# Fewer, longer loads of the first queries, and a new deal of decoding and narrow copies between VectorE and ScalarE, in a causal attention with an MLP behind it

## The chip, the cores and the metric

One core of a Trainium2 chip runs the whole program. Its engines are TensorE (PE in the rows; PEld is its weight load), VectorE (DVE), ScalarE (ACT), GpSimd (POOL) and SyncE (SP), which here only issues transfers (SPq). The metric is device time in microseconds (us), median of several runs; lower is better. A measurement of this kernel can tell about 0.2% (1.2 us) from no change.

## The reference

```
scores = q @ k^T / sqrt(64), causal mask            # batch 4, heads 12, seq 448, dim 64
attn   = softmax(scores);  x = attn @ v             # -> 1792 tokens x 768
h = x @ w_in                                        # 768 x 2048
g = max(h, 0) + alpha * min(h, 0)
out = g @ w_out                                     # 2048 x 768
```

Everything is float32. The weights and v reach the kernel as 64-bit words, so w_in has to be decoded on the chip.

## The kernel before, in words

**Attention** works on 24 pairs of heads (p = 0 to 23). A loop of iterations n runs the steps of several pairs side by side: in iteration n a step written `NAME+lag` in the text `ORDER` (or in `ROUNDS` for the first n) is done for pair n - lag. The text is the order in which every engine's instructions are issued, and each engine takes its own in that order. The steps of one pair:

- `LK`, `LQ` (`load`): SP's loads of keys and queries, two transfers each, one for each head of the pair. The first 64 query rows go into a tile of their own, `qd` (two more transfers). `LW` loads `vd`, the v rows for the 64-row half blocks; `LV` loads pieces of v. `ST` stores finished x.
- `S0`, `S1`, `S2` (`scores`): TensorE. `MXij` (`row_max`): VectorE, mask and row extreme in PSUM. `EXij` (`row_exp`): ScalarE. `RC` (`row_rec`, the lines `sm` and `rs` in the rows): VectorE's reciprocal of the row sums. `NOij` (`row_norm`): the seven scalings on GpSimd, which start when RC is done.
- `PT0` to `PT2`, and `PTH` (`transpose_halves`, the half blocks): transposes on TensorE into PSUM. `C00` to `C30` (`pt_copy`): copies of them to SBUF. The last letter says which engine copies: a ScalarE, d VectorE. `C00` and `C30` are the narrow ones (128x256).
- `AV`, `AH`: attention times v on TensorE; `AH` needs `C30`. `XF`, `XH`, `XL`: sums and splits of x out of PSUM.

`E2`, `EH`, `EG`, `ED`, `EA` are places in the order at which other work is run, taken from the table `EARLY`, which has a list for each n. The words of it: `LD` loads a piece of w_in (SP, into one buffer `raw`, free again when the piece before is decoded); `A`, `I` (ScalarE), `C` (GpSimd), `D` (VectorE: `p_shift` and `p_sign`) and `+` (GpSimd, in two halves) decode piece 0, 1, 2; `S`, `cast`, `sub` make weight operands; `h` and `l` split x into a high part (GpSimd) and a low part (VectorE, line L725); `4` is a GpSimd sum. Most of them run at `ED`, near the end of the iteration; `A`, `I` and `cast` at `EA`, after it; `D` at `EG`, ahead of `XF` and `RC`.

**The MLP** starts inside the last iterations (`begin_block`, `go_on`, `last_of_it` of the hooks) and then runs as a planned list, with TensorE busy throughout.

Of the kernel before, what the change touches and what calls it, by code (L numbers as in the profile page):

```python
# [11 lines left out]
F32 = mybir.dt.float32  # L12
# [181 lines left out]
def kernel(  # L194
# [269 lines left out]
    def load(p, nm, eng=nc.sync, also=None):  # L464

        b, hp = pairs[p]
        o = LQ if nm == "q" else 0
        T[nm, p] = ap["in"].tile([P, S - o], F32, tag=nm + "r", name=f"{nm}r_{p}")
        src = {"q": qt, "k": kt}[nm][b, hp]
        for j in range(2):  # L470
            (also if j and also else eng).dma_start(out=T[nm, p][half(j)], in_=src[:, j, o:])
        if nm == "q":
            for j in range(2):
                eng.dma_start(out=qd[p % 3][half(j), j * LQ : (j + 1) * LQ], in_=src[:, j, :LQ])

# [60 lines left out]
    def scores(p, n):  # L536

        if n == 2:  # L540
# [94 lines left out]
    def pt_copy(p, i, j, eng):  # L635
# [290 lines left out]
    with tc.manual_schedule():  # L926
# [601 lines left out]
```

## Time and profile before

| | |
|---|---|
| median of 3 runs | 596.08 us (595.0 to 596.35) |
| the profiled execution | 596.71 us, of which the span from first to last instruction is 594.9 |
| PE busy, whole span | 571.3 us, 96% |
| DVE, ACT, POOL busy | 464.9, 393.0, 288.8 us |
| mean granted TensorE clock | 0.983 of 2.4 GHz |

A row of the timeline reads: start in us, length in us, engine, line, operation, what it writes and reads, how many of its kind are merged in it, and in square brackets how long the engine was idle before it and what ended that.

### The profile page before, as it was taken

To read this page: it belongs to the slowest core of one execution; us is meant where nothing else is said; L and a number is where in the kernel's file an instruction comes from. 1 tells how busy PE (TensorE), PEld (TensorE's weight loads), DVE (VectorE), ACT (ScalarE), POOL (GpSimd) and SP (SyncE) were. 2 spreads that over 40 slices of the span, in tenths; PEclk is the share of its full clock that TensorE was granted. 3 is DMA by queue.
4 is the path that set the end of the run, shared out by engine and by line. 5 is a ranking of instruction groups with operands and counts; after the bars stand their busy time and mean duration, and the time that the engine had idled before them with its cause. 6 is when DMAs were issued, how large, how long until landed. Compare 5 with 4: busy or idle time off the path is not lost.

```text
span 594.9 us, 11547 instructions
## 1 busy us (share of the span) xinstructions
PE 571.3 (96%) x3921; PEld 504.6 (85%) x3921; DVE 464.9 (78%) x975; ACT 393.0 (66%) x921; POOL 288.8 (49%) x334
## 2 busy tenths in 40 slices
PE   8998799879998999999999999999989999999997
PEld 4766567556687999999999999999979999999997
DVE  5886688858966977767886778887997899897763
ACT  6886889759967757556664754777676566565431
POOL 7665378777662434435444531533444453456420
PEclk9899799979999999999999999999999999999999
DMA  5755554553233676575676757395452325403533
GB/s 153 193 154 134 133 142 132 163 143 98 82 89 136 215 235 222 216 252 212 214 255 210 231 205 249 128 333 194 125 151 71 105 66 150 141 9 118 178 100 113
DMA packets 94586, 95.92 MB, mean 161 GB/s; under 512 B 24608, under 2 KB 83648, under 8 KB 94528
## 3 DMA queue, kind: packets, MB, share of 16 engines
q1 hardware_dynamic: 93680, 93.65, 51.0%
q0 software_dynamic: 528, 1.08, 0.7%
q8 instruction: 31, 0.51, 0.4%
q10 hardware_dynamic: 320, 0.46, 0.2%
q14 instruction: 27, 0.22, 0.1%
HBM read 66.85 MB, written 28.31 MB: 160 GB/s over the span
## 4 chain that ended last, share of the span: by engine, by line
PE 64%; DVE 4%; issue 1%; ACT 0%; DVEq 0%
PE bank L406 33%; PE bank L1321 30%; DVE x1l L1299 1%; DVE dec L1289 1%; DVE x1h L1258 0%; DVE dec L1247 0%; DVE wo L1258 0%; DVE tf L1289 0%; DVE acc L1457 0%; DVE wie L1258 0%; DVE acc L323 0%; PE bank L657 0%; DVE acc L1289 0%; DVE tf L1334 0%; DVE acc L319 0%
## 5 line engine op out<-in xcount | busy, mean ns | idle before, releaser
L528 POOL TENSOR_SCALAR p<-p,rs 128x192 f32<-128x192 f32 (+3 forms) x164 | 86.1, 546 | 54.9 <-DVE rs L599 35.9
L1321 PE MATMUL bank<-x1h,x1l 128*128 128x384 f32 x540 | 98.7, 335 | 1.0 <-DVE x1h L1258 0.9
L1321 PEld LDWEIGHTS bank<-x1h,x1l 128*128 128x128 f32 x540 | 94.3, 188 | 1.6 <-DVE x1h L1258 1.2
L585 ACT ACTIVATE p<-bank,nm 128x320 f32<-128x320 f32 (+3 forms) x168 | 82.1, 496 | 18.1 <-DVE nm L570 18.0
L570 DVE CUSTOM_DVE_ANT_0 bank<-bank,mask 128x320 f32<-128x320 f32 (+3 forms) x168 | 72.3, 478 | 22.0 <-ACT p L585 12.4
L430 ACT ACTIVATE tf<-bank 128x448 f32<-128x448 f32 x64 | 34.4, 543 | 41.9 <-PE bank L406 30.5
L557 PE MATMUL bank<-kr,qr 64*128 64x320 f32 (+2 forms) x288 | 51.7, 471 | 0.5 <-ACT x1h L524 0.5
L434 DVE SCALAR_TENSOR_TENSOR tf<-tf,om,bank 128x448 f32<-128x448 f32 x64 | 41.7, 674 | 7.7 <-ACT tf L430 7.3
L406 PE MATMUL bank<-x1h,wir 128*128 128x448 f32 x192 | 44.6, 368 | 0.0
L630 PE MATMUL bank<-ident,p 128*128 128x128 f32 x288 | 40.9, 294 | 1.4 <-POOL p L528 1.3
L1321 PE MATMUL bank<-x1h,gset 128*128 128x384 f32 x216 | 40.4, 338 | 0.9 <-DVE acc L1334 0.9
L524 ACT ACTIVATE ptf<-bank 128x384 f32<-128x384 f32 (+1 forms) x94 | 38.9, 470 | 2.0 <-PE bank L630 1.6
L649 PE MATMUL bank<-ptf,v 128*64 128x128 f32 (+2 forms) x288 | 35.7, 382 | 3.8 <-DMA v<-in_v_dram 3.8
L1321 PEld LDWEIGHTS bank<-x1h,gset 128*128 128x128 f32 x216 | 37.9, 188 | 1.2 <-ACT acc L1455 1.2
L406 PEld LDWEIGHTS bank<-x1h,wir 128*128 128x128 f32 x192 | 36.0, 188 | 3.3
L630 PEld LDWEIGHTS bank<-ident,p 128*128 128x128 f32 x288 | 33.9, 149 | 4.6 <-POOL p L528 2.8
L557 PEld LDWEIGHTS bank<-kr,qr 64*128 64x128 f32 x288 | 28.8, 198 | 10.6 <-ACT p L585 3.2
L329 POOL TENSOR_TENSOR dec<-dec,tf 128x768 int32<-128x768 int32 x11 | 22.0, 1996 | 30.6 <-ACT tf L430 16.5
L420 DVE TENSOR_TENSOR bank<-bank,tf 128x448 f32<-128x448 f32 x30 | 18.9, 630 | 22.1 <-PE bank L406 20.9
L1299 POOL TENSOR_TENSOR x1l<-acc,x1l 128x512 fp32r<-128x512 f32 x12 | 16.4, 1368 | 40.6 <-ACT x1l L1295 31.7
L585 ACT ACTIVATION_READ_ACCUMULATOR p<-bank,nm 128x1 f32 x168 | 33.7, 201 | 0.0
L406 PE MATMUL bank<-x1h,wie 128*128 128x448 f32 x144 | 33.4, 367 | 0.0
(195 smaller groups left out, 1387.1 us busy)
## 6 DMA issues: line engine op xcount, KB each, us to landing
gd<-tf SPq DMA_DIRECT2D x64, 224.0 KB, 2.1
tf<-gd SPq DMA_DIRECT2D x28, 256.0 KB, 4.5
acc<-gd SPq DMA_DIRECT2D x28, 256.0 KB, 4.3
dec<-in_moe_w_in_dram SPq DMA_DIRECT2D x9, 768.0 KB, 4.9
tf<-in_moe_w_in_dram SPq DMA_DIRECT2D x7, 768.0 KB, 4.8
dec<-in_moe_w_out_dram SPq DMA_DIRECT2D x7, 768.0 KB, 4.7
tf<-in_moe_w_out_dram SPq DMA_DIRECT2D x7, 768.0 KB, 4.6
dec<-wd SPq DMA_DIRECT2D x13, 384.0 KB, 4.6
```

The costliest lines, as they stand in the source:

```text
L406: nc.tensor.matmul(ps, w[:, u, k * P : (k + 1) * P], x[:, k], start=(st in ("P1", "P5") and i == 0), stop=(i == len(mms) - 1), skip_group_ ...
L430: nc.scalar.activation(t, bank_of(g, b, role), AF.Relu, scale=-1.0)
L434: stt(out=t, in0=t, scalar=om[:, f : f + 1], in1=bank_of(g, b, role), op0=ALU.mult, op1=ALU.add)
L524: eng.activation(out, x, AF.Copy, scale=side)
L528: eng.tensor_scalar(out=out, in0=x, scalar1=side, scalar2=1.0, op0=ALU.mult, op1=ALU.mult)
L557: nc.tensor.matmul(ps[:, o : o + lim], T["q", p][half(j), i * QP : (i + 1) * QP], T["k", p][half(j), :lim], start=(o == 0), stop=(n > 0 or ...
L570: nc.vector.tensor_tensor_reduce(out=t, in0=t, in1=mask_of(i), scale=-SCALE, scalar=MOST_F32, op0=ALU.add, op1=ALU.min, accum_out=nm,)
L585: nc.scalar.activation(T["p", p, i][:, j, : t.shape[1]], t, AF.Exp, scale=-1.0, bias=T.pop(("nm", p, i, j)), accum_out=T["sm", p][:, z : z ...
L630: nc.tensor.transpose(ps[:, j - js[0], c], t[:, j, c * QP : (c + 1) * QP], T["ident"])
L649: nc.tensor.matmul(out[half(j), c * QP + LQ :], vs[b % 2][:, hp, c, j], x[:, : (NQ - c) * QP], start=(c == 0), stop=False, skip_group_chec ...
L1299: eng.tensor_tensor(out=x[:, 4 * P :], in0=g_of(p, nm), in1=x[:, : 4 * P], op=ALU.subtract)
L1321: nc.tensor.matmul(ps, x, w, start=(st in ("P1", "P5")[: 1 if Q else 2] and i == 0), stop=(i == len(mms) - 1), skip_group_check=True,)
```

## The change

1. `load`: the first queries of three pairs come in one pair of transfers, at every third pair, into one of two larger `qd` tiles, instead of two transfers for every pair. On SP 16 rows of two transfers go away.
2. `p_sign` may work on half a piece (`G`), and each half stands in the iteration of its `+`. Pieces 0 and 1 are decoded about one iteration later; the second `LD` moves from n = 8 to n = 9, and its `A` from 9 to 10. `S`, `l` and all of `D`, `G` now run at `EG`, ahead of `XF` and `RC`.
3. `attention`: in twelve iterations `C00`, and in five of these `C30` too, is copied by VectorE instead of ScalarE. Early `LW` and `MX1` move behind other steps.
4. For the last pair (p = 23) `PTH` runs in n = 26 with its other transposes, in a bank it shares with PT0, and VectorE copies its `C30` there.

```
-    4: "A:0", 5: "I:0 C:0", 6: "D:0", 7: "D:0 +:0:0", 8: "+:0:1 LD", 9: "A:1", 10: "I:1 C:1", 11: "D:1 h", 12: "D:1 h l",
-    13: "+:1:0 h", 14: "+:1:1 4 h LD", 15: "4 h", 16: "S:S1 S:S2 l 4 h", 17: "S:S3 l l h cast:A11", 18: "l l h sub:A11 cast:S1",
-    19: "sub:S1 l h cast:S2", 20: "sub:S2 l h A:2", 21: "S:S4 l h C:2", 22: "l h I:2", 23: "l", 24: "l",
+    4: "A:0", 5: "I:0 C:0", 7: "D:0", 8: "G:0:0 +:0:0", 9: "G:0:1 +:0:1 LD", 10: "A:1", 11: "I:1 C:1 h", 12: "h", 13: "D:1 h",
+    14: "G:1:0 +:1:0 h 4", 15: "G:1:1 +:1:1 4 h LD", 16: "l l l 4 h", 17: "S:S1 S:S2 l h cast:A11", 18: "S:S3 l l h sub:A11 cast:S1",
+    19: "l sub:S1 h cast:S2", 20: "l sub:S2 h A:2", 21: "S:S4 l h C:2", 22: "l h I:2", 23: "l", 24: "l",
...
-    def p_sign(key):
-        y = line(ys[key]).bitcast(I32)
-        stt(out=y, in0=parts_of(key)[1], scalar=-0x40000000, in1=y, op0=ALU.bitwise_and, op1=ALU.bitwise_or)
+    def p_sign(key, part=None):
+        y, high = line(ys[key]).bitcast(I32), parts_of(key)[1]
+        if part is not None:
+            y, high = y[:, :, part * P : part * P + P], high[:, :, part * P : part * P + P]
+        stt(out=y, in0=high, scalar=-0x40000000, in1=y, op0=ALU.bitwise_and, op1=ALU.bitwise_or)
...
-        if nm == "q":
+        if nm == "q" and p % 3 == 0:
+
             for j in range(2):
-                eng.dma_start(out=qd[p % 3][half(j), j * LQ : (j + 1) * LQ], in_=src[:, j, :LQ])
+                eng.dma_start(
+                    out=qd[p // 3 % 2][half(j), :, j * LQ : (j + 1) * LQ],
+                    in_=qt[b, hp : hp + 3, :, j, :LQ].rearrange("h d s -> d h s"),
+                )
...
-        T["both", p] = bank("pt", p, NQ, 0, uses=2 if p + 2 < edge[1] else 1)
-        ps = T["pt", p, NQ, 0] = T["both", p][:, : 2 * QP].rearrange("p (j c n) -> p j c n", j=2, c=1)
+        if p == edge[1]:
+
+            ps = held["pt", p, 0, 0][0][:, 2 * QP :]
+            held["pt", p, 0, 0][1] += 1
+        else:
+            T["both", p] = bank("pt", p, NQ, 0, uses=2 if p + 2 < edge[1] else 1)
+            ps = T["both", p][:, : 2 * QP]
+        ps = T["pt", p, NQ, 0] = ps.rearrange("p (j c n) -> p j c n", j=2, c=1)
...
-        first[26] = order_of(ORDER.replace("C10+3a ", "").replace("EH+4 ", "EH+4 C10+3a "))
+
+        for n in (5, 6, 10, 11, 12, *range(17, 23)):
+            text = ORDER.replace("C00+3a", "C00+3d")
+            if n in (5, 6, 11, 12, 21):
+                text = text.replace("C30+4a ", "").replace("MX20+2 ", "MX20+2 C30+4d ")
+            first[n] = order_of(text)
+        first[1], first[4] = order_of(ORDER.replace("LW+1 ", "")), order_of(ORDER.replace("C00+3a", "C00+3d").replace("LW+1", "LW+2 LW+1"))
+
+        text = ORDER.replace("C10+3a ", "").replace("EH+4 ", "EH+4 C10+3a ").replace("PT2+3 ", "PT2+3 PTH+3 ")
+        first[26] = order_of(text.replace("C21+3d ", "C21+3d C30+3d "))
+        first[27] = order_of(ORDER.replace("PTH+4 ", "").replace("C30+4a ", ""))
...
-                    rear = to is plan and kind in ("A", "I", "cast") and n < len(pairs)
-                    fns = (behind_it if rear else to).setdefault(n, [])
+
+                    home = {"D": gap, "G": gap, "l": gap, "S": gap, "A": behind_it, "I": behind_it, "cast": behind_it}
+                    fns = (home.get(kind, to) if to is plan and n < len(pairs) else to).setdefault(n, [])
...
-        for n in range(3):
-            qd.append(ap["mk"].tile([P, 2 * LQ], F32, name=f"qd{n}"))
+        for n in range(2):
+            qd.append(ap["mk"].tile([P, 3, 2 * LQ], F32, name=f"qd{n}"))
```

**SP, the loads of n = 17 and 18 (pairs 17 and 18), before.** `kr` and `qr` are keys and queries, `xd` a store of x; the last two v pieces, `v1`, are the ones that AV reads from n = 19 on.

```order
L471 DMA kr_17_1627<-in_k_dram 64x448 x2
L471 DMA qr_17_1630<-in_q_dram 64x384 x2
L474 DMA qd2_104<-in_q_dram 64x64 x2
L506 DMA v1_171<-in_v_dram 96x6x128
L506 DMA v1_171<-in_v_dram 32x6x128
L498 DMA vd0_173<-in_v_dram 64x4x64 x2
L705 DMA xd_B11_80<-tf_74 128x448
L471 DMA kr_18_1729<-in_k_dram 64x448 x2
L471 DMA qr_18_1732<-in_q_dram 64x384 x2
L474 DMA qd0_100<-in_q_dram 64x64 x2
L506 DMA v1_171<-in_v_dram 80x6x128
L506 DMA v1_171<-in_v_dram 48x6x128
```

The same place on SP in the changed kernel:

```order
L473 DMA kr_17_1604<-in_k_dram 64x448 x2
L473 DMA qr_17_1607<-in_q_dram 64x384 x2
L512 DMA v1_169<-in_v_dram 96x6x128
L512 DMA v1_169<-in_v_dram 32x6x128
L504 DMA vd0_171<-in_v_dram 64x4x64 x2
L717 DMA xd_B11_80<-tf_74 128x448
L473 DMA kr_18_1704<-in_k_dram 64x448 x2
L473 DMA qr_18_1707<-in_q_dram 64x384 x2
L477 DMA qd0_100<-in_q_dram 64x3x64 x2
L512 DMA v1_169<-in_v_dram 80x6x128
L512 DMA v1_169<-in_v_dram 48x6x128
```

The `qd` load of n = 17 is gone; that of n = 18 has become one for three pairs. The same goes for the 24 pairs: 8 such rows are left.

**VectorE from the end of n = 16 to the first row maximum of n = 17, before** (`sm`, `rs`: RC; `L354`: the sums S; `L725`: a low part l; `L570`: MX):

```order
L570 ISA bank6_67,nm_14_3_0_1562<-bank6_67,mask64_150 128x64
L570 ISA nm_14_3_0_1562 128x1
L598 TENSOR_TENSOR sm_14_1534<-sm_14_1534,least_69 128x7
L599 RECIPROCAL rs_14_1584<-sm_14_1534 128x7
L526 COPY ptf_13_1606<-bank7_68 128x3x128
L354 TENSOR_TENSOR dec_77<-dec_77 128x384 x2
L725 TENSOR_TENSOR x1l_73<-tf_74,x1h_72 128x448
L570 ISA bank3_64,nm_15_1_0_1622<-bank3_64,mask448_149 128x320
```

And in the changed kernel:

```order
L576 ISA bank4_65,nm_15_3_0_1639<-bank4_65,mask64_148 128x64
L576 ISA nm_15_3_0_1639 128x1
L356 TENSOR_TENSOR dec_77<-dec_77 128x384 x2
L737 TENSOR_TENSOR x1l_73<-tf_74,x1h_72 128x448
L604 TENSOR_TENSOR sm_15_1611<-sm_15_1611,least_69 128x7
L605 RECIPROCAL rs_15_1664<-sm_15_1611 128x7
L532 COPY ptf_14_1686<-bank0_61 128x2x128
L532 COPY ptf_14_1686<-bank1_62 128x3x128
L576 ISA bank6_67,nm_16_1_0_1699<-bank6_67,mask448_147 128x320
```

The two sums and the low part stood between RC and the next MX, in n = 16; now they stand ahead of RC, one iteration later, and a narrow copy (`128x2x128`) stands behind it.

**TensorE, the last pair's transposes, before** (`L406`: MLP steps; `L621`: PTH; `L649`: AV):

```order
L630 MATMUL bank4_65<-ident_144,p_23_2_2455 128x128 x3
L406 MATMUL bank6_67<-x1h_72,wir_2425 128x448 x6
L406 MATMUL bank6_67<-x1l_73,wir_2425 128x448 x3
L406 MATMUL bank0_61<-x1h_72,wir_2425 128x448 x6
L406 MATMUL bank0_61<-x1l_73,wir_2425 128x448 x3
L621 MATMUL bank3_64<-ident_144,p31_172 64x64 x2
L621 MATMUL bank3_64<-ident_144,p_23_0_2447 64x64 x2
L621 MATMUL bank3_64<-ident_144,p_23_1_2433 64x64 x2
L621 MATMUL bank3_64<-ident_144,p_23_2_2455 64x64 x2
L649 MATMUL bank1_62<-ptf_23_2599,v0_169 64x384 x2
```

And in the changed kernel:

```order
L642 MATMUL bank4_65<-ident_142,p_23_2_2423 128x128 x3
L633 MATMUL bank1_62<-ident_142,p31_170 64x64 x2
L633 MATMUL bank1_62<-ident_142,p_23_0_2415 64x64 x2
L633 MATMUL bank1_62<-ident_142,p_23_1_2401 64x64 x2
L633 MATMUL bank1_62<-ident_142,p_23_2_2423 64x64 x2
L408 MATMUL bank6_67<-x1h_72,wir_2393 128x448 x6
L408 MATMUL bank6_67<-x1l_73,wir_2393 128x448 x3
L408 MATMUL bank0_61<-x1h_72,wir_2393 128x448 x6
L408 MATMUL bank0_61<-x1l_73,wir_2393 128x448 x3
L661 MATMUL bank3_64<-ptf_23_2575,v0_167 64x384 x2
```

The half blocks' transposes now stand two MLP steps ahead of AV.

## Rows read from the trace of the kernel before

**Rows 1.** Windows of 10 us: busy of each engine, PEclk, DMA share, GB/s.

```profile
60.00:70.00 10.00, 7.19 (x66) 5.54 (x68) 5.47 (x23) 8.64 (x27) 4.20 (x8) 0.66 0.54 137
120.00:130.00 10.00, 6.20 (x64) 4.93 (x62) 4.26 (x18) 5.76 (x21) 5.91 (x12) 0.75 0.56 146
250.00:260.00 10.00, 10.00 (x50) 9.18 (x50) 7.02 (x12) 6.23 (x11) 5.46 (x4) 1.00 0.89 293
```

**Rows 2.** Timeline of SP's queue, at three places in the attention.

```profile
54.80 0.47 SPq L289 DMA_DIRECT2D dec<-in_moe_w_in_dram  x1
...
74.92 1.20 SPq L471 DMA_DIRECT2D kr<-in_k_dram  x2
76.17 1.23 SPq L471 DMA_DIRECT2D qr<-in_q_dram  x2
77.45 1.24 SPq L474 DMA_DIRECT2D qd<-in_q_dram  x2
...
80.25 1.35 SPq L498 DMA_DIRECT2D vd<-in_v_dram  x2
...
121.14 1.12 SPq L506 DMA_DIRECT2D v<-in_v_dram  x2
```

**Rows 3.** Timeline, 48 to 75 us, all engines: the first gap.

```profile
51.01 1.02 POOL L329 TENSOR_TENSOR dec<-dec 128x384 int32<-128x384 int32 x1
...
60.08 0.89 ACT L307 ACTIVATE dec<-dec 128x768 f32<-128x768 f32 x1 [5.55 <-DMA dec<-in_moe_w_in_dram]
...
62.81 1.13 PE L657 MATMUL bank<-ptf,vd 128*64 128x64 f32 x16 [4.94 <-ACT ptf L524]
```

**Rows 4.** Timeline, 115 to 135 us, all engines: the second gap.

```profile
125.72 0.69 PE L649 MATMUL bank<-ptf,v 128*64 128x128 f32 x4 [3.80 <-DMA v<-in_v_dram]
```

**Rows 5.** Timeline of DVE: RC of n = 5, 6, 8, 10, 11, 16, 17, 18, 19, 20.

```profile
28.53 0.20 DVE L599 RECIPROCAL rs<-sm 128x7 f32<-128x7 f32 x1
34.57 0.20 DVE L599 RECIPROCAL rs<-sm 128x7 f32<-128x7 f32 x1
...
47.30 0.20 DVE L599 RECIPROCAL rs<-sm 128x7 f32<-128x7 f32 x1
...
65.00 0.20 DVE L599 RECIPROCAL rs<-sm 128x7 f32<-128x7 f32 x1
72.62 0.20 DVE L599 RECIPROCAL rs<-sm 128x7 f32<-128x7 f32 x1
...
103.66 0.20 DVE L599 RECIPROCAL rs<-sm 128x7 f32<-128x7 f32 x1
111.01 0.20 DVE L599 RECIPROCAL rs<-sm 128x7 f32<-128x7 f32 x1
118.34 0.20 DVE L599 RECIPROCAL rs<-sm 128x7 f32<-128x7 f32 x1
128.11 0.20 DVE L599 RECIPROCAL rs<-sm 128x7 f32<-128x7 f32 x1
136.77 0.20 DVE L599 RECIPROCAL rs<-sm 128x7 f32<-128x7 f32 x1
```

**Rows 6.** Timeline of DVE, 13 to 15 and 103 to 105 us.

```profile
13.80 0.42 DVE L526 COPY ptf<-bank 128x256 f32<-128x256 f32 x1
...
103.39 0.17 DVE L598 TENSOR_TENSOR sm<-sm,least 128x7 f32<-128x7 f32 x1 [0.94 <-ACT p L585]
...
104.20 1.57 DVE L354 TENSOR_TENSOR dec<-dec 128x384 f32<-128x384 f32 x2
```

**Rows 7.** Timeline, 183 to 200 us: the last pair's half blocks.

```profile
185.94 0.36 ACT L524 ACTIVATE ptf<-bank 128x256 f32<-128x256 f32 x1
...
186.36 0.69 PE L657 MATMUL bank<-ptf,vd 128*64 128x64 f32 x16 [1.55 <-ACT ptf L524]
```

**Rows 8.** Groups by line and form, 15 to 185 us (busy, mean ns).

```profile
L323 DVE SCALAR_TENSOR_TENSOR dec<-dec 128x768 int32<-128x768 int32 x3 | 3.2, 1058 | 0.0
...
L524 ACT ACTIVATE ptf<-bank 128x256 f32<-128x256 f32 x46 | 17.7, 386 | 0.1
```

More of the change, by code (lines that the diff above doesn't have):

```diff
@@ L44 @@
 ROUNDS = {2: """
-LK+0 LQ+0 EX10+2 EX11+2 MX00+2 EX00+2 MX01+2 EX01+2 MX20+2 EX20+2 MX21+2 EX21+2 RA+2 NO10+2p NO11+2p NO00+2p NO01+2p MX30+2 S0+1 S1+1 PT1+2 PT0+2 MX10+1 MX11+1 EX30+2 RB+2 LW+1 NO20+2p NO21+2d NO30+2p
+LK+0 LQ+0 EX10+2 EX11+2 MX00+2 EX00+2 MX01+2 EX01+2 MX20+2 EX20+2 MX21+2 EX21+2 RA+2 NO10+2p NO11+2p NO00+2p NO01+2p MX30+2 S0+1 S1+1 PT1+2 PT0+2 MX10+1 MX11+1 EX30+2 RB+2 NO20+2p NO21+2d NO30+2p
 """, 3: """
-LK+0 LQ+0 EX10+2 EX11+2 MX00+2 EX00+2 MX01+2 EX01+2 MX20+2 S2+2 EX20+2 MX21+2 PT2+3 EX21+2 C00+3d C20+3a C21+3d C10+3d S0+1 S1+1 SF+1 LW+1 MX30+2 MX10+1 EX30+2 MX11+1 RC+2 NO10+2p NO11+2p NO00+2p NO01+2p NO20+2p NO21+2d NO30+2p
+LK+0 LQ+0 EX10+2 EX11+2 MX00+2 EX00+2 MX01+2 EX01+2 MX20+2 S2+2 EX20+2 MX21+2 PT2+3 EX21+2 C00+3d C20+3a C21+3d C10+3d S0+1 S1+1 SF+1 LW+3 LW+2 MX30+2 EX30+2 RC+2 NO10+2p NO11+2p NO00+2p NO01+2p NO20+2p NO21+2p NO30+2p MX10+1 MX11+1
 """}
@@ L548, in scores @@
             for j in range(2):
-                nc.tensor.matmul(ps[half(j)], qd[p % 3][:, half(j)], T["k", p][:, :LQ], start=True, stop=True)
+                nc.tensor.matmul(ps[half(j)], qd[p // 3 % 2][:, p % 3, half(j)], T["k", p][:, :LQ], start=True, stop=True)
             T["s", p, NQ, 0] = ps
@@ L639, in pt_copy @@
         copy(T["ptf", p][:, j : j + t.shape[1], SLOTS[i]], t, eng)
-        bank_done("pt", p, i, j)
+        bank_done("pt", p, 0 if p == edge[1] and i == NQ else i, j)
     def av(p):
@@ L806, in plan_early @@
                     kind, *arg = w.split(":")
-                    rear = to is plan and kind in ("A", "I", "cast") and n < len(pairs)
-                    fns = (behind_it if rear else to).setdefault(n, [])
+                    home = {"D": gap, "G": gap, "l": gap, "S": gap, "A": behind_it, "I": behind_it, "cast": behind_it}
+                    fns = (home.get(kind, to) if to is plan and n < len(pairs) else to).setdefault(n, [])
                     if kind == "D":
-                        key = piece_names[int(arg[0])]
-                        bits.setdefault(key, iter([lambda key=key: p_shift(key), lambda key=key: p_sign(key)]))
-                        (gap if to is plan and n < 25 else to).setdefault(n, []).append(lambda key=key: next(bits[key])())
+                        fns.append(lambda key=piece_names[int(arg[0])]: p_shift(key))
+                    elif kind == "G":
+                        fns.append(lambda key=piece_names[int(arg[0])], part=int(arg[1]): p_sign(key, part))
                     elif kind == "LD":
@@ L829, in plan_early @@
                         fns.append(lambda f=f, key=piece_names[int(arg[0])]: f(key))
-    bits = {}
     def pool(stack, name, side="left"):
```

## The prediction

> **What bounds the kernel now.** I read the windows first, to see where TensorE does not work all the time. In the MLP it does: the window from 250 to 260 us has PE busy for all 10 us at a granted clock of 1.00 [rows 1]. What is saved before the MLP is therefore passed on in full, and nothing in the change touches the MLP. In the attention two windows stand out, with PE busy for 7.19 and 6.20 of 10 us and a granted clock of 0.66 and 0.75, that is, part of the time on the lower of its two levels, 1.2 instead of 2.4 GHz [rows 1].
>
> The timeline names both gaps. In the first, ScalarE stood still for 5.55 us ahead of `A` of the second weight piece, until its transfer landed at 60.08; TensorE then lost 4.94 us ahead of `AH`, since the copies that it needs stand behind `A` on ScalarE [rows 3]. In the second, TensorE lost 3.80 us because a v piece had not landed [rows 4].
>
> Why were these transfers late? SP's queue tells it. The buffer of the weight piece came free when GpSimd's addition ended, at 51.01 + 1.02 = 52.03 [rows 3], but SP issued the load only at 54.80; the v pieces left at 121.14 and were wanted 0.8 us later, at 125.72 - 3.80 = 121.92 [rows 2, 4]. In between SP issues without a pause: the rows from 74.92 follow each other within 0.1 us. An ordinary iteration costs it 1.20 + 1.23 + 1.24 + 1.35 = 5.0 us for keys, queries, `qd` and `vd`, and about 1.1 to 1.4 more where two v pieces are added, plus 0.05 between rows: some 6.4 us [rows 2]. The loop itself needs 34.57 - 28.53 = 6.04 us per iteration, from one `RC` to the next [rows 5]. So with v loads the queue is slower than the loop that it feeds, and falls behind.
>
> Third, the intervals between the `RC` rows show what an iteration loses: 7.35 and 7.33 us at n = 16 and 17 (103.66, 111.01, 118.34), 9.77 and 8.66 around the second gap (to 128.11 and 136.77), 7.62 behind the first (65.00 to 72.62) [rows 5]. Last comes the end of the attention: `AH` of the last pair waits 1.55 us for its narrow copy on ScalarE [rows 7].
>
> **The change, part by part.**
>
> *The qd loads.* 16 of 24 rows go, 16 x 1.24 = 20 us of SP's queue [rows 2]; the 8 that are left move three times the bytes in as many transfers, and I take 1.35 for each, as for the `vd` row, which is also one transfer of several blocks per row. An iteration then costs SP some 3.9 us, with v 5.2, with `qd` 6.5 in every third: less than 6.04 on the mean, so SP no longer lags but waits for buffers. The Trainium skill ("DMA: Bandwidth & Descriptors", Rules for kernel authors) says the same more strongly: below 64 KB a transfer is mostly overhead, and its Anatomy section, on transfers that GpSimd issues, puts the fixed part at about 2 us. As an estimate from that page, 32 transfers of 16 KB would give 64 us if each paid it in turn; the rows show 0.62 us of issue each with the rest overlapped, so the sum goes by the 20 us, and those only matter where SP was late.
>
> *First gap.* The load no longer waits for SP, but it still waits for GpSimd. The `+` stays one iteration ahead of `A`; only both move by one. GpSimd ended the addition 52.03 - 47.30 = 4.73 us after the `RC` of its iteration, and the load takes 60.08 - 54.80 = 5.28, so it lands 10.1 us behind that `RC`, with 0.1 for the issue. ScalarE reached `A` at 60.08 - 5.55 = 54.53, 7.2 us behind the same `RC`, and without the `C00` ahead of it comes 0.2 to 0.4 earlier [rows 3, 5, 8]. A wait of 3.1 us is left, of 5.55: 2.45 gained. The gap also took TensorE to its low clock, and the next interval lasted 7.62, 1.58 above the plain one. TensorE's gap was 0.6 shorter than ScalarE's, so about 2.4 us are left of it; the 1.55 us at the end of the attention cost no clock [rows 7], the 3.80 us did [rows 4, 1]. Being nearer to the first, I count the 1.58 as gained. Together -4.0. Bounds: -1.5 (the load takes its longest, the clock falls) and -7.1 (no wait).
>
> *Second gap.* Now the v pieces of n = 18 wait only for what stands ahead of them: the store of n = 17, which needs ScalarE's `XH`, then keys, queries, `qd`: 0.6 + 1.2 + 1.25 + 1.35 + 0.55, so the last is issued some 5 us after the `XH` of n = 17. They took up to 125.72 - 121.14 = 4.6 us from the first one's issue [rows 2, 4], so they are there by 9.5. TensorE wants them in n = 19, at 121.92 - 111.01 = 10.9 us behind the `RC` of n = 17, or 9.6 to 10.2 with shorter intervals. It just fits. Gained: 3.80, and 136.77 - 128.11 - 6.04 = 2.62 of low clock behind it: -6.4. Bounds: -3 (0.8 us late and part of the low clock) and -6.4.
>
> *S and l moved to `EG`.* At the old place each delayed the next row maximum: two S (1.57 together) and an l made n = 16 lose 7.35 - 6.04 = 1.31, and n = 17 lost 1.29. At the new one they first fill the 0.94 us for which VectorE waited for ScalarE's last exponential ahead of `RC` [rows 6], but then push `RC`, GpSimd's scalings and the next copies. For n = 16, 17, 18 with some 1.85 us each (three operations of 0.6) about 0.9 sticks out of the 0.94, of which 0.3 to 0.4 is absorbed ahead of the next row maximum: 0.5 each, 0.3 more with a copy behind `RC` in two of them, 2.1 against the old 2.6. In n = 19 to 25, where x sums already fill that place, I take 0.7 lost. Net +0.2. Bounds: -2.6 (all hidden) and +5 (12 l and 4 S, half of their 10 us paid beyond the old price).
>
> *Shift and halves of sign.* A sign costs 1.06 whole [rows 8], some 0.55 a half. At n = 8, 9 they take the place that whole ones had. At n = 13 to 15 they stand beside two x sums each and a split, where VectorE has no pause: +1.0, bounds 0 and +1.6 (all three in full).
>
> *Copies.* 18 narrow copies leave ScalarE (386 ns each, [rows 8]) for VectorE (420 ns, [rows 6]). Twelve of them stand behind `RC`, where VectorE has 0.3 to 0.4 us before TensorE's new scores; the five `C30` delay `MX21` and `AH`, against a ScalarE that has `A`, `I` or `cast` to do there. I take 0.1 for each of five: +0.5. Bounds: -2 and +7.6 (18 x 0.42, nothing hidden).
>
> *Early loads, larger memsets, first row maxima*: hidden behind the first scores, within 0.5 either way, taken as 0; without that cover a memset twice as long costs 0.2.
>
> *Last pair.* `PTH` is off the place ahead of `AV`, its copy is done two MLP steps earlier, and `AH` follows `AV`: -1.55 [rows 7]. Bounds -0.5 (another input is next) and -1.8.
>
> Sum: -4.0 - 6.4 + 0.2 + 1.0 + 0.5 - 1.55 = -10.25. The profiled execution, 594.9 of span and 1.8 around it, 596.7, becomes 586.45; the median of the runs lies 0.6 below it. Predicted: 585.8.
>
> **Rivals.**
> - *The first gap stays.* Nothing in the change loads the piece sooner against `A`, only SP is out of the way. If SP, now waiting in its queue for GpSimd, still sends it late, or TensorE's shorter gap takes the clock down all the same, the -4.0 is lost: 589.8. For it: GpSimd's 4.73 is untouched. Against: 2.8 us of the 5.55 are SP's alone.
> - *VectorE pays half.* Copies and moved operations cost half of their bounds: some 3.8 for copies and 2.5 for S and l, less the 0.7 counted: +5.6, 591.4. For it: 0.94 is the widest pause that VectorE had. Against: in both windows of the gaps it was busy about half the time [rows 1].
> - *Slower.* All that is moved ahead of `RC` or behind it is paid in full: copies 7.6, S and l 16 x 0.6 to 0.78 less the 3 that the old place cost, 6.6 to 9.5: with +1.6 that is 15.8 to 18.7 against 12 gained, 600 to 603. It decides from about three quarters of that price. Against it: the pauses of VectorE that rows 6 show, and ScalarE's lighter load.
> - *No change.* The transfers are late on the rings, not in the queue; both gaps stay, the tail gains, VectorE loses its 1.7: 596. The Trainium skill speaks for it ("DMA: Bandwidth & Descriptors", Specifications): a transfer needs pieces of 512 bytes for full rate, and 64 elements of a `qd` row remain 256. Against it: the DMA share of the two windows is 0.54 and 0.56, and 0.89 in the MLP's [rows 1].
> - *Better.* The load meets `A`, or S and l are hidden whole: 581.5.
>
> **How the numbers follow.** Forecast (582.5 to 588.5) 0.60; first gap stays 0.16; VectorE pays half 0.10; better 0.06; no change 0.04; slower 0.04. All but the last two are faster by more than the 0.2% (1.2 us) that can be told from no change: 0.92, 0.04, 0.04. For 8 in 10 the range must take in the first rival and the better case: 581 to 591.
>
> **What would show it.** Right: SP's queue has pauses from some 15 us on; the load of the second piece follows GpSimd's addition within 0.2 us, and ScalarE waits about 3 us ahead of `A`; the granted clock stays at 1.00 from 50 to 70; no wait on v near 115; `RC` intervals of 6.5 to 6.9 for n = 16 to 18; `AH` of the last pair waits for nothing, and the MLP begins 10 us sooner at the same length. Wrong: TensorE waits for narrow copies of VectorE, intervals over 6.5 where `C30` moved, v that still lands late, or a clock of 0.66 behind a gap of 2 us.

## The result and the profile after

The changed kernel takes 591.75 us (median of 7 runs, 588.45 to 592.47) against 596.35 on the same chip. The ratio, taken over all executions and not from the two medians, is 0.9907, 95% interval 0.988 to 0.9933. The kernel is faster, as forecast, but by 4.6 us in the medians and 5.6 us by the ratio, where 10.3 were forecast. Its median lies 0.75 above the range's upper end of 591, the mean of its runs (590.9) just inside. The executions that are compared below took 590.37 us (span 588.6) and, before, 596.71 (594.9): 6.3 us of span.

Windows of 10 us of the changed kernel, columns as in [rows 1]:

```profile
50.00:60.00 10.00, 10.00 (x126) 7.49 (x123) 8.53 (x33) 9.40 (x36) 6.62 (x12) 1.00 0.30 73
60.00:70.00 10.00, 7.03 (x82) 4.92 (x81) 6.23 (x24) 7.31 (x21) 4.52 (x10) 1.00 0.94 243
120.00:130.00 10.00, 7.92 (x83) 5.92 (x84) 6.41 (x22) 5.81 (x21) 6.47 (x12) 0.83 0.61 154
```

TensorE still has two gaps, but in the first the granted clock stayed at 1.00 in this execution (before 0.66). The timeline of VectorE gives the `RC` of n = 9 to 12 and 15 to 20, to be set against [rows 5]:

```profile
53.69 0.20 DVE L605 RECIPROCAL rs<-sm 128x7 f32<-128x7 f32 x1
59.81 0.20 DVE L605 RECIPROCAL rs<-sm 128x7 f32<-128x7 f32 x1
68.49 0.20 DVE L605 RECIPROCAL rs<-sm 128x7 f32<-128x7 f32 x1
74.88 0.20 DVE L605 RECIPROCAL rs<-sm 128x7 f32<-128x7 f32 x1
...
95.08 0.20 DVE L605 RECIPROCAL rs<-sm 128x7 f32<-128x7 f32 x1
103.51 0.20 DVE L605 RECIPROCAL rs<-sm 128x7 f32<-128x7 f32 x1 [0.46 <-DVE sm L604]
110.23 0.20 DVE L605 RECIPROCAL rs<-sm 128x7 f32<-128x7 f32 x1
116.35 0.20 DVE L605 RECIPROCAL rs<-sm 128x7 f32<-128x7 f32 x1
123.76 0.20 DVE L605 RECIPROCAL rs<-sm 128x7 f32<-128x7 f32 x1
131.90 0.20 DVE L605 RECIPROCAL rs<-sm 128x7 f32<-128x7 f32 x1
```

By stages: from n = 4 to 12 the change won 3.9 us (78.77 - 22.13 before, 74.88 - 22.15 after); from 12 to 16 it lost 3.7 (103.66 - 78.77 against 103.51 - 74.88), 2.4 of it in n = 16 alone (8.43 for 6.04); from 16 to 20 it won 4.7 (33.11 became 28.39), where some 7 had been forecast; from 20 to 25 it lost 0.2, and behind that it won 1.6.

The first gap in the timeline, all engines: GpSimd's addition, the load that waits for it, ScalarE's `A`, TensorE's `AH`.

```profile
57.38 1.03 POOL L331 TENSOR_TENSOR dec<-dec 128x384 int32<-128x384 int32 x1
58.44 0.39 SPq L289 DMA_DIRECT2D dec<-in_moe_w_in_dram  x1
63.29 0.91 ACT L307 ACTIVATE dec<-dec 128x768 f32<-128x768 f32 x1 [2.47 <-DMA dec<-in_moe_w_in_dram]
66.59 0.69 PE L669 MATMUL bank<-ptf,vd 128*64 128x64 f32 x16 [2.97 <-DVE ptf L532]
```

The load left 0.03 us after the addition, and ScalarE waited 2.47 instead of 5.55 [rows 3]. TensorE waited 2.97, and what ended that was `C30` of n = 11, which the change gave to VectorE; with the copies back on ScalarE (number 7) it waited 2.14. The second gap, on SP, GpSimd and TensorE:

```profile
89.44 1.29 SPq L504 DMA_DIRECT2D vd<-in_v_dram  x2
99.83 0.39 SPq L289 DMA_DIRECT2D dec<-in_moe_w_in_dram  x1
100.31 1.13 SPq L473 DMA_DIRECT2D kr<-in_k_dram  x2
...
111.56 0.55 SPq L717 DMA_DIRECT2D xd_B<-tf  x1
...
117.56 0.86 SPq L512 DMA_DIRECT2D v<-in_v_dram  x2
...
98.78 1.02 POOL L331 TENSOR_TENSOR dec<-dec 128x384 int32<-128x384 int32 x1
...
108.42 0.55 ACT L530 ACTIVATE tf<-bank 128x448 f32<-128x448 f32 x1
...
122.08 0.44 PE L661 MATMUL bank<-ptf,v 128*64 128x128 f32 x4 [2.62 <-DMA v<-in_v_dram]
```

Here is what the forecast did not see. The third weight load waits for the addition that ends at 98.78 + 1.02 = 99.80, and everything behind it in SP's queue waits with it: from 89.44 + 1.29 = 90.73 to 99.83 SP issues nothing. After that no pause between two rows is longer than 0.4 us up to the last v pieces at 117.56. The store of n = 17 shows the backlog: its `XH` ended at 108.42 + 0.55 = 108.97, it left at 111.56, 2.6 us later. In the kernel before, the same load had stopped the queue too, for 3.1 us, from 91.45 + 1.34 = 92.79 to 95.88:

```profile
91.45 1.34 SPq L498 DMA_DIRECT2D vd<-in_v_dram  x2
95.88 0.39 SPq L289 DMA_DIRECT2D dec<-in_moe_w_in_dram  x1
```

The prediction had read the queue as issuing "without a pause" from 54.80 to 121.14, so this wait could have been read before the run. With fewer rows SP comes to it sooner and stands longer. The Trainium skill ("DMA: Bandwidth & Descriptors", Anatomy of one DMA) says, in a section on transfers that GpSimd issues, that DMA engines do not wait on semaphores and that a wait is spent on the issuing sequencer ahead of dispatch. The rows of SP agree, with 9.1 us.

### The profile page after: what moved, and what is told of

It reads as the page before. It is cut to its first block, busy times and chain, and to the rows that moved or that the text cites. A ratio compares the mean times of both kernels' runs of the same rounds, so it can differ in the third digit from the quotient of the medians.

```text
span 588.6 us, 11532 instructions
## 1 busy us (share of the span) xinstructions
PE 569.9 (97%) x3921; PEld 503.2 (85%) x3921; DVE 471.6 (80%) x993; ACT 389.7 (66%) x903; POOL 285.1 (48%) x335
## 4 chain that ended last, share of the span: by engine, by line
PE 72%; DVE 15%; ACT 6%; issue 2%; DMA 2%; POOL 1%; SPq 1%; DVEq 0%; ACTq 0%; POOLq 0%
PE bank L408 35%; PE bank L1342 32%; DVE bank L576 5%; ACT p L591 5%; PE bank L642 2%; DVE ptf L532 2%; PE bank L563 1%; DVE tf L693 1%; DVE x1l L737 1%; DVE nm L576 1%; POOL p L534 1%; DMA dec<-in_moe_w_in_dram 1%; DVE x1l L723 1%; PE bank L669 1%; DMA v<-in_v_dram 1%
## 5 line engine op out<-in xcount | busy, mean ns | idle before, releaser
L534 POOL TENSOR_SCALAR p<-p,rs 128x320 f32<-128x320 f32 (+3 forms) x165 | 81.0, 515 | 54.3 <-DVE rs L605 43.2
L576 DVE CUSTOM_DVE_ANT_0 bank<-bank,mask 128x320 f32<-128x320 f32 (+3 forms) x168 | 72.6, 477 | 19.4 <-ACT p L591 10.3
L563 PE MATMUL bank<-kr,qr 64*128 64x448 f32 (+2 forms) x288 | 53.7, 474 | 0.0
L642 PE MATMUL bank<-ident,p 128*128 128x128 f32 x288 | 38.8, 284 | 1.5 <-POOL p L534 1.4
L642 PEld LDWEIGHTS bank<-ident,p 128*128 128x128 f32 x288 | 32.1, 143 | 4.5 <-POOL p L534 2.9
L530 ACT ACTIVATE ptf<-bank 128x256 f32<-128x256 f32 (+2 forms) x76 | 33.3, 486 | 2.8 <-PE bank L642 1.6
```

Of the source, the lines that this page charges most:

```text
L530: eng.activation(out, x, AF.Copy, scale=side)
L534: eng.tensor_scalar(out=out, in0=x, scalar1=side, scalar2=1.0, op0=ALU.mult, op1=ALU.mult)
L563: nc.tensor.matmul(ps[:, o : o + lim], T["q", p][half(j), i * QP : (i + 1) * QP], T["k", p][half(j), :lim], start=(o == 0), stop=(n > 0 or ...
L576: nc.vector.tensor_tensor_reduce(out=t, in0=t, in1=mask_of(i), scale=-SCALE, scalar=MOST_F32, op0=ALU.add, op1=ALU.min, accum_out=nm,)
L642: nc.tensor.transpose(ps[:, j - js[0], c], t[:, j, c * QP : (c + 1) * QP], T["ident"])
```

## The experiments

Each was timed against the kernel before on the same chip (median 596.81 for the first four, 597.25 for the next four, 597.06 for the last four). These three groups ran on three chips: between kernels of two groups, a difference of medians and one worked out from the ratios come out up to 1 us apart.

**1. The third load one iteration later** (e1).

```diff
-15: "G:1:1 +:1:1 4 h LD", 16: "l l l 4 h"
+15: "G:1:1 +:1:1 4 h", 16: "l l l 4 h LD"
```

> Only the third weight load LD moves from n = 15 to n = 16, behind that iteration's k, q, v and vd loads on SP. Theory Q (head of the line: SP stood from 90.7 to 99.83 us behind this load's wait for GpSimd, and everything after it, the last v pieces too, is late by what it then has to catch up): the 2.62 us gap of TensorE ahead of AV at n = 19 goes, the clock stays up there, RC 18 to RC 20 falls from 15.55 to 12 to 13 us; span 588.6 - 3 to 4.5 = 584 to 585.6, median 587 to 589. Rival V (the v pieces are late by their own chain: store, keys, queries, qd, v): the load's place changes nothing, the gap is 2 to 2.6 us, span about 588.6, median 591.75.

589.68 us, ratio 0.988 (0.9866 to 0.9894). TensorE no longer waits for v, and `RC` goes from 118.14 (n = 18) to 130.34 (n = 20), 12.2 us instead of 15.55. SP's queue:

```profile
101.79 0.39 SPq L289 DMA_DIRECT2D dec<-in_moe_w_in_dram  x1
...
110.79 0.36 SPq L717 DMA_DIRECT2D xd_B<-tf  x1
...
115.99 0.85 SPq L512 DMA_DIRECT2D v<-in_v_dram  x2
```

and ScalarE's `XH` ahead of that store:

```profile
110.22 0.55 ACT L530 ACTIVATE tf<-bank 128x448 f32<-128x448 f32 x1
```

Now SP is ahead: the store leaves 0.02 us after its `XH`, and the v pieces 5.2 us after it, as forecast. The wait at the head of the queue was the cause. Only 2 of the 3.3 us arrive in the median, 0.7 short of what was expected; in this profile the clock fell behind the first gap (n = 11 and 12: 8.51 and 8.00), which may be the rest.

**2. The v pieces one iteration sooner, the load left alone** (e2).

```diff
-12: 2, 13: 2, 14: 2
+11: 2, 12: 2, 13: 2
```

> Only the last six v pieces are issued one iteration earlier (n = 15, 16, 17 instead of 16, 17, 18). Both Q and V: no wait on v at n = 19, worth the 2.62 us and the low clock behind it, 3 to 4.5 us of span, median 587 to 589. If the gap goes but the span falls by less than 2.6, something else ends those iterations (VectorE's sums and low parts).

589.56, ratio 0.9873 (0.9857 to 0.9889); no wait for v, n = 18 to 20 in 12.22. The same gap goes by another way, though n = 15 now takes 8.01 instead of 6.90.

**3. `A` of the second piece one iteration later** (e3).

```diff
-10: "A:1", 11: "I:1 C:1 h", 12: "h"
+11: "A:1 h", 12: "I:1 C:1 h"
```

> Only A of the second weight piece moves from n = 10 to 11 and I, C from 11 to 12, so that its load has an iteration more. Theory G (what is left of the first gap, 2.47 us of ScalarE and 2.97 of TensorE, is the load's own 4.85 us behind GpSimd's addition): no wait ahead of A, RC 10 to RC 11 falls from 8.68 to 6.1 to 6.5; span 585.9 to 586.3. Theory K (the runs of the changed kernel spread from 588.4 to 592.5 because the clock falls in some of them behind the first gap and not in others): the runs also come closer together, within 2 us. Rival: the work of A, I, D crowds n = 11 to 13 and takes back 1 us or more.

587.79 (586.09 to 591.04), ratio 0.9852 (0.9828 to 0.9876). `A` finds its piece, n = 11 takes 6.26 instead of 8.68. The runs still spread over 5 us, where 2 had been expected: the second gap, left alone here, has the clock of its window at 0.83.

**4. Two low parts instead of three in n = 16** (e4).

```diff
-12: "h", ... 16: "l l l 4 h"
+12: "h l", ... 16: "l l 4 h"
```

> Only one of the three low parts l of n = 16 moves to n = 12. Theory L (the interval to RC 16, 8.43 us against 6.04 before, is the three low parts, 2.96 us beside GpSimd's sum, ahead of RC, and ScalarE's XH waiting for one of them): that interval falls by 0.9 to 1.3, n = 12 pays at most 0.4; span down by 0.5 to 1.3. Rival: the interval is GpSimd's (addition, sum, high part and seven scalings, 6.1 us in a row), and stays above 8.

590.71, ratio 0.9904 (0.9879 to 0.9929), no different from the changed kernel in time, where 0.5 to 1.3 us had been expected; but n = 16 took 7.38 instead of 8.43. The rows of the changed kernel on VectorE, GpSimd and ScalarE say why:

```profile
100.01 1.89 DVE L737 TENSOR_TENSOR x1l<-tf,x1h 128x448 fp32r<-128x448 f32 x1
101.83 1.15 DVE L737 TENSOR_TENSOR x1l<-tf,x1h 128x448 fp32r<-128x448 f32 x2
...
99.76 1.14 POOL L752 TENSOR_TENSOR tf<-tf 128x448 f32<-128x448 f32 x1
100.87 0.57 POOL L534 TENSOR_SCALAR x1h<-tf 128x448 fp32r<-128x448 f32 x1
...
102.00 0.54 ACT L530 ACTIVATE tf<-bank 128x448 f32<-128x448 f32 x1 [0.94 <-DVE x1l L737]
...
109.51 0.61 DVE L737 TENSOR_TENSOR x1l<-tf,x1h 128x448 fp32r<-128x448 f32 x1
```

Of the three low parts, 2.96 us together, the first lies beside GpSimd's sum and high part and takes 1.89; the other two take 0.61 each, as one alone does at 109.51. ScalarE's `XH`, which overwrites what they read, waits for them. The Trainium skill ("SBUF — State Buffer", Who interferes with whom) says that a VectorE instruction with two SBUF inputs contends with a GpSimd instruction that reads SBUF; this is such a pair, and the rows agree, with 1.89 against 0.61.

**5. The merged first queries alone, on the kernel before** (e5).

```diff
-        if nm == "q":
+        if nm == "q" and p % 3 == 0:
```

(with the longer transfer and the two larger tiles that go with it)

> The kernel before with one part of the change alone: the first queries of three pairs loaded together; all else as before, the second and third loads at n = 8 and 14. Theory Q (SP's queue made both transfers late; in the whole change the third load, one iteration later, put its wait for GpSimd at the head of SP's queue): here SP has no lag and stands for GpSimd one iteration sooner than in the changed kernel, so both gaps shrink: ScalarE waits about 2.5 to 3 us ahead of A of the second piece instead of 5.55, and the second gap is gone (RC from n = 18 to 20 about 12.2 instead of 18.43). Time 596.35 - 2.8 - 6.4 = 587.2, 585.6 with the clock behind the first gap. Rival: the merged load does little by itself, and the 4.6 us come from the moved decoding and copies: 594 or more.

586.22 (584.69 to 589.94), ratio 0.9831 (0.9799 to 0.9862): by the ratios one part of the change gives 10.1 us (11.0 by the medians), and all the rest takes back 4.5 of it (0.0076 of 597). The new tiles also hold the first queries of six pairs instead of three. A free tile was not what the loads had lacked: in the trace of the kernel before, the waits of SP's queue from 14 to 140 us have no entry for the `qd` loads (L474). The timeline of number 5 on SP, ScalarE and TensorE, in an execution of 589.73:

```profile
51.73 0.39 SPq L289 DMA_DIRECT2D dec<-in_moe_w_in_dram  x1
...
56.43 0.91 ACT L307 ACTIVATE dec<-dec 128x768 f32<-128x768 f32 x1 [2.21 <-DMA dec<-in_moe_w_in_dram]
...
59.17 0.71 PE L661 MATMUL bank<-ptf,vd 128*64 128x64 f32 x16 [2.33 <-ACT ptf L528]
...
120.24 0.44 PE L653 MATMUL bank<-ptf,v 128*64 128x128 f32 x4 [2.29 <-DMA v<-in_v_dram]
```

Both waits are shorter than in the changed kernel (2.97 and 2.62). The second gap is not gone, as I had expected: SP stands for GpSimd in n = 14 here, until 91.93, and does not make it up in four iterations. The six executions sort by the mean granted clock: 584.69 and 584.71 us at 1.000 and 0.999, 585.82 and 586.62 at 0.997 and 0.996, 589.73 and 589.94 at 0.988.

**6. The changed kernel with first queries for each pair again** (e6), the reverse of 5.

```diff
-        if nm == "q" and p % 3 == 0:
+        if nm == "q":
```

> The changed kernel with two transfers of first queries for every pair again. Theory Q: SP lags again. Four more rows of 1.24 us stand between the third load and the last v pieces of n = 18, less what waits anyway: the second gap grows from 2.6 to some 6 us, the first by up to 2.8 with its clock: 591.75 + 3.5 + 2.8 = 598 (595 to 601). Rival, the rest of the change carries the gain: within 1.5 us of 591.75.

598.92, ratio 1.0031 (1.0011 to 1.0052): without the merged loads the rest of the change is a loss, of 1.9 us. SP lags again:

```profile
61.49 0.47 SPq L289 DMA_DIRECT2D dec<-in_moe_w_in_dram  x1
...
67.23 0.89 ACT L307 ACTIVATE dec<-dec 128x768 f32<-128x768 f32 x1 [5.36 <-DMA dec<-in_moe_w_in_dram]
...
129.13 0.69 PE L657 MATMUL bank<-ptf,v 128*64 128x128 f32 x4 [4.61 <-DMA v<-in_v_dram]
```

The second gap is 4.61 us, where some 6 had been expected.

**7. The changed kernel with the narrow copies of its iterations back on ScalarE** (e9).

```diff
-            text = ORDER.replace("C00+3a", "C00+3d")
-            if n in (5, 6, 11, 12, 21):
-                text = text.replace("C30+4a ", "").replace("MX20+2 ", "MX20+2 C30+4d ")
```

(and the same for the `C00` of n = 4)

> The changed kernel with the narrow copies of the loop's iterations (C00 in twelve, C30 in five) back on ScalarE; the last pair's stay with VectorE. Prediction's term: the copies cost 0.5, so 591.2, the same within what can be told. Rival, VectorE pays half: 588. Rival, ScalarE needs the room: the first gap keeps its 2.5 us and ScalarE gets late ahead of RC in n = 11, 12 and 17 to 22: 593 to 596.

587.35 (586.45 to 590.14), ratio 0.9847 (0.9823 to 0.9872), nearest to the rival "VectorE pays half". `RC` from n = 4 to 25 is 3.5 us shorter, 1.6 of it in n = 20, where the clock stayed up this time.

**8. Moves 1, 3 and 4 together** (e10).

```diff
-10: "A:1", 11: "I:1 C:1 h", 12: "h", ... 15: "G:1:1 +:1:1 4 h LD", 16: "l l l 4 h"
+11: "A:1 h", 12: "I:1 C:1 h l", ... 15: "G:1:1 +:1:1 4 h", 16: "l l 4 h LD"
```

> The changed kernel with three moves together: third load in n = 16, A of the second piece in n = 11 (I and C in n = 12), one of the three low parts of n = 16 in n = 12. Theories Q, G and L: no wait on v (RC 18 to 20 about 12.2), no wait for A (n = 11 about 6.3, n = 12 6.4 to 6.8), n = 16 about 7.4. By the sum of the intervals, 591.75 - 3.3 - 2.4 - 1 = 585, and, if the falls of the clock behind the two gaps are what spreads the changed kernel's runs, with runs that lie within 1.5 us. Rival: the moves give their gains back elsewhere, 587.5 or more.

584.24 (583.15 to 584.55), ratio 0.9782 (0.9761 to 0.9803): 7.5 us below the changed kernel with three kinds of entries of the table moved, and runs within 1.4 us. The loop runs at 6.13, 6.24 and 6.34 in n = 10 to 12 and 12.2 for n = 19 and 20; nothing waits for a transfer. Without these gaps the spread is small, so numbers 9 to 11 take this kernel as their start. They ran on another chip, so a single term is read to some 1 us, and the intervals are given beside it.

**9. Number 8 with the narrow copies on ScalarE** (e11), by the edit of number 7:

```diff
-            text = ORDER.replace("C00+3a", "C00+3d")
```

> The kernel with the three moves, and the narrow copies of its iterations (C00 in twelve, C30 in five) back on ScalarE. Theory V (VectorE pays for the copies; the 3.5 us that came back without them in the changed kernel were 1.8 of copies and 1.6 of a clock that did not fall): 584.24 - 1.8 = 582.4, with n = 5, 6 and 7 0.3 to 0.4 shorter each and n = 12 about 0.3. Rival, all 3.5 to 4.4 us are copies: 580 to 580.7. Rival, the prediction's 0.5: 583.7 or more.

581.51 (581.19 to 583.35), ratio 0.9751 (0.9727 to 0.9775): the copies on VectorE cost 2.7 us by the medians and 1.9 by the ratios. This is the fastest kernel of the study, 15.5 us below the one before. The intervals of n = 6 and 7 went from 6.54 and 6.21 to 6.11 and 5.88. That of n = 5 did not fall as expected, it rose from 6.45 to 7.73: the profiled execution is the slowest of the five (583.35), and in it TensorE waited twice for `vd`, and the granted clock was 0.50 from 22 to 24 us.

```profile
18.90 0.30 PE L669 MATMUL bank<-ptf,vd 128*64 128x64 f32 x2 [1.03 <-DMA vd<-in_v_dram]
20.48 0.68 PE L669 MATMUL bank<-ptf,vd 128*64 128x64 f32 x14 [1.28 <-DMA vd<-in_v_dram]
```

With n = 5 taken from number 7 (6.03), the intervals of n = 5 to 25 give 135.00 - 133.93 + 7.73 - 6.03 = 2.8 us for the copies.

**10. Number 8 with S and l at `ED` again** (e13).

```diff
-home = {"D": gap, "G": gap, "l": gap, "S": gap, "A": ...
+home = {"D": gap, "G": gap, "A": ...
```

> The kernel with the three moves, with S and l back at ED, near the iteration's end, as before. Prediction's term: the new place costs 0.2, so 584.0. The intervals of n = 16 to 25 add up to 64.2 here, and to 64.2 in the kernel before with plain intervals in the second gap's place: the same, 583.2 to 585.2. Rival, the place ahead of RC is the dearer one: 582 or less; the other rival, that it is a gain: 586 or more, with 7.3 in n = 17 and 18.

586.46 (586.2 to 586.87), ratio 0.9829 (0.9805 to 0.9854): the new place is a gain of 2.2 us (2.8 by the ratios, 1.7 by the intervals of n = 5 to 25), the second rival. The place behind `RC` costs twice. On TensorE and GpSimd, n = 17:

```profile
106.54 4.52 POOL L534 TENSOR_SCALAR p<-p,rs 128x320 f32<-128x320 f32 x7 [0.80 <-DVE rs L605]
...
111.44 0.69 PE L669 MATMUL bank<-ptf,vd 128*64 128x64 f32 x16 [1.47 <-ACT ptf L530]
```

and in number 8:

```profile
107.50 3.37 POOL L534 TENSOR_SCALAR p<-p,rs 128x320 f32<-128x320 f32 x7 [1.44 <-DVE rs L605]
...
110.57 0.69 PE L669 MATMUL bank<-ptf,vd 128*64 128x64 f32 x16 [0.94 <-ACT ptf L530]
```

Behind `RC`, S and l delay the row maxima (the first starts 2.68 us behind `RC` of n = 17, instead of 0.87) and also lie beside GpSimd's seven scalings, which take 4.52 instead of 3.37. The new place has its price too: the two S of n = 17, now beside GpSimd's sum, take 2.10 us in number 8 and 1.35 here.

**11. Number 8 with the last pair's half blocks as before** (e14).

```diff
-        text = ORDER.replace("C10+3a ", "").replace("EH+4 ", "EH+4 C10+3a ").replace("PT2+3 ", "PT2+3 PTH+3 ")
-        first[26] = order_of(text.replace("C21+3d ", "C21+3d C30+3d "))
-        first[27] = order_of(ORDER.replace("PTH+4 ", "").replace("C30+4a ", ""))
+        first[26] = order_of(ORDER.replace("C10+3a ", "").replace("EH+4 ", "EH+4 C10+3a "))
```

(and `PTH` of the last pair again in a bank of its own)

> The kernel with the three moves, with the last pair's half blocks after the MLP steps, and copied by ScalarE, as before. Prediction's term: 584.24 + 1.55 = 585.8, with AH of the last pair waiting 1.55 us. Rival, the wait goes and something else of the end takes its place: 584.3.

586.06 (585.17 to 586.78), ratio 0.9821 (0.9798 to 0.9843): 1.8 us (2.3 by the ratios), and the old wait is back:

```profile
175.92 0.69 PE L669 MATMUL bank<-ptf,vd 128*64 128x64 f32 x16 [1.55 <-ACT ptf L530]
```

**12. Built up from the kernel before** (e12): merged queries, the last pair's order, and in its table:

```diff
-9: "A:1", 10: "I:1 C:1", 11: "D:1 h", 12: "D:1 h l", 13: "+:1:0 h", 14: "+:1:1 4 h LD", ... 16: "S:S1 S:S2 l 4 h"
+10: "A:1", 11: "I:1 C:1 h", 12: "D:1 D:1 h", 13: "+:1:0 h l", 14: "+:1:1 4 h", ... 16: "S:S1 S:S2 l 4 h LD"
```

> Built up from the kernel before instead: the merged first queries, the last pair's half blocks with its others, A of the second piece one iteration later (n = 10; I and C 11; both of D 12) and the third load in n = 16; S, l, the whole sign and all narrow copies as before. By the intervals of the merged loads alone: 586.2 less 3.5 (first gap: 8.41 and 7.35 become 6.1 each), 3.5 (second gap: 7.62 and 8.12 become 12.2 together) and 1.55 (end), plus 0.9 for a shift and a sign in one iteration: 578.6. Rival, what the merged loads gain is given back once the gaps go, because VectorE or ScalarE is next: 581 or more.

583.03 (582.79 to 583.19), ratio 0.9772 (0.9748 to 0.9796). The expectation was 4.4 too low, and mostly by its bookkeeping: the intervals came from an execution of 589.73 and were taken from the median of 586.22. From 589.73 the same sum gives 582.1. Both gaps are gone (n = 10 and 11: 5.95 and 6.08); n = 12, with shift and sign together, costs 7.34, 1.3 above the plain one instead of 0.9, and n = 17 and 18, with S and l at `ED`, 7.34 and 7.32.

## Why the prediction was off

The step that failed is the one on the **second gap**, "It just fits", with -6.4. The gap gave 2.9 (from `RC` of n = 18 to that of n = 20: 18.43 before, 15.55 after), just outside the bound of 3. The premise "now the v pieces of n = 18 wait only for what stands ahead of them" named the store, keys and queries, but not the weight load, which stands in the same queue ahead of them, waits for GpSimd, and is moved by the change from n = 14 to 15. Number 1 shows that premise and sum hold as soon as the load is out of the way: v 5.2 us behind `XH`, no wait. With the load ahead of them the v pieces left 8.6 us behind `XH` (117.56 - 108.97), 3.4 later: 2.6 of backlog, and 0.8 because the rows from the store to them took 6.0 us instead of 5.2. TensorE waited 2.62. Queue time was counted (20 us of rows less); that it is worth nothing while the queue stands was not.

| term | forecast | measured |
|---|---|---|
| first gap | -4.0 | -4.3 in this execution (n = 10 to 12: 25.51 to 21.19), 1.3 to 1.6 less where the clock falls |
| second gap | -6.4 | -2.9 |
| S and l moved | +0.2 | -2.2 (number 10; -1.7 by the intervals), +1.05 for the third l of n = 16 (number 4) |
| shift and halves of sign | +1.0 | +1.35 (n = 13 to 15: 18.85 to 20.20), by intervals only |
| copies | +0.5 | +2.7 (number 9; 1.9 by the ratios) |
| last pair | -1.55 | -1.6 by the intervals; -1.8 (number 11) |

The right-hand column (with -1.6 for the last pair) adds up to -5.9, beside 6.3 of span. Its rows overlap, so that this is no proof of them: by numbers 8 and 9, 0.7 us of the copies lies in n = 10 to 12 and 0.7 in n = 19 and 20, that is, in the rows of the two gaps. That the forecast came as near as it did is in part luck: S and l came out 1.35 better than forecast in sum and the copies 2.2 worse, so that the two errors in part cancel and the whole is off by little more than the second gap's 3.5. Early loads and memsets, taken as 0, cost nothing (`RC` of n = 4 at 22.13 before, 22.15 after).

**First gap:** the mechanism was right to the place (2.47 of wait for 3.1 forecast, load 0.03 us behind the addition), though TensorE's gap was 2.97 instead of the 2.4 counted. That the clock would stay was right in the execution shown and wrong in others, so this part of the -4.0 is luck: with the same gap, numbers 1 and 4 took 8.00 and 7.69 in n = 12 for the 6.39 here. **S and l** had the sign wrong: I priced what they push ahead of `RC`, but at the old place only the row maximum, not GpSimd's scalings. The three low parts of n = 16 were priced at 0.6 us each; one took 1.89, and n = 16 took 8.43 where 6.5 to 6.9 had been forecast.

**Copies:** the twelve `C00`, put at nothing, were the error, not the five `C30`. In n = 5, 6 and 7 the interval is 6.44, 6.54 and 6.22, for 6.03, 6.09 and 5.88 in number 7, and in n = 7 no `C30` has moved. The rows from `RC` of n = 6 to the first row maximum, in the changed kernel:

```profile
35.13 0.20 DVE L605 RECIPROCAL rs<-sm 128x7 f32<-128x7 f32 x1
...
35.84 0.88 DVE L532 COPY ptf<-bank 128x256 f32<-128x256 f32 x2
36.64 0.49 DVE L576 CUSTOM_DVE_ANT_0 bank<-bank,mask 128x320 f32<-128x320 f32 x1
```

and in number 7:

```profile
34.28 0.20 DVE L605 RECIPROCAL rs<-sm 128x7 f32<-128x7 f32 x1
...
34.98 0.55 DVE L532 COPY ptf<-bank 128x384 f32<-128x384 f32 x1
35.45 0.49 DVE L576 CUSTOM_DVE_ANT_0 bank<-bank,mask 128x320 f32<-128x320 f32 x1
```

With `C00` the row maximum starts 1.51 us behind `RC`, without it 1.17: 0.34 of the copy's 0.42 shows. Between numbers 8 and 9 these delays of eleven iterations (n = 4 left out) add up to 2.8 us. The pause of 0.3 to 0.4 us that was to hide the copy is there in few of them: in number 9 VectorE waits for scores ahead of that row maximum in n = 10, 11, 12 and 20 (0.35 to 0.49 us), and not in n = 5, 6, 17 to 19, 21 and 22. `C30` of n = 6, between two later row maxima, adds 0.11 (from the first row maximum behind `RC` of n = 5 to `RC` of n = 6: 5.03 us for 4.92), as forecast, although TensorE's `AH` waits for it:

```profile
32.76 0.42 DVE L532 COPY ptf<-bank 128x256 f32<-128x256 f32 x1
...
33.23 0.69 PE L669 MATMUL bank<-ptf,vd 128*64 128x64 f32 x16 [0.55 <-DVE ptf L532]
```

**Last pair:** right. `AH` follows `AV` without a wait. Three of the prediction's own signs of being wrong were there: TensorE waiting for narrow copies of VectorE, an interval over 6.5 where `C30` moved (6.54 in n = 6), and v that landed late.

Of the rivals, "VectorE pays half" gave 591.4 and is near in time, but not in its parts: it had the copies at 3.8 (2.7 measured), S and l at 2.5 (a gain), and the second gap closed. "No change" by the length of the pieces falls with numbers 5 and 6: 16 merged transfers in place of 48, with the same pieces of 256 bytes, gave 10 us alone, and the rest of the change without them lost 1.9.

Open stays a part of the 4.5 us (by the ratios) between the changed kernel and number 5. The terms above make 1.1 (copies, sign and third l, less S and l and the last pair), the longer waits of both gaps 1.0 (2.97 - 2.33 + 2.62 - 2.29). The other 2.4 may be the clock, which fell in more executions of the changed kernel (mean 0.987 to 0.997 in seven) than of number 5 (0.988 twice, 0.996 or more in four); what decides it in an execution was not found.

## What to carry to other kernels

In these traces a transfer that waited at the head of SP's queue held back all transfers behind it, for 3.1 to 9.1 us. When a load is moved, look for the wait it carries and for the next urgent transfer behind it, and put the load where its buffer is already free. Where a change has several parts, time alone the part on which the largest terms rest: here it was worth 10.1 us by the ratios, and the whole 5.6. A copy of 0.4 us on a busy engine is free only where a row shows a pause at that very place; here four of eleven places had one. Take intervals and total from one execution, not intervals from a profile and the total from a median.

## What was not expected of the hardware

Behind gaps of TensorE of 2.1 to 3.2 us the granted clock fell in some executions and stayed in others, and the length of the gap alone does not decide it: in the profile of number 5 it fell behind gaps of 2.33 and 2.29 us (0.69 and 0.66 in the 5 us from 60 and from 120), in that of number 7 it stayed at 1.00 behind 2.14 and 2.88. Number 5 ran 584.7 us at a mean of 1.00 and 589.9 at 0.988. With the gaps gone (number 8) the runs lie within 1.4 us.

The same pair of engines slows on either side: GpSimd's seven scalings grew from 3.37 to 4.52 us beside VectorE's sums and a low part (number 10), and a low part from 0.61 to 1.89 beside GpSimd's sum and high part (number 4).
